# The last batch's down projection as seven products over pairs of d_ff blocks, in an attention and bilinear feed-forward kernel

## The chip, the core and the metric

The kernel is one program on one core of a Trainium2 chip. The core has five engines with queues of their own: TensorE (PE, matrix products into PSUM), VectorE (DVE), ScalarE (ACT), GpSimd (POOL) and SyncE (SP, which here only issues transfers). PEld in a profile is PE's loading of weights, beside its products. Each engine takes its instructions in the order in which the program lists them and waits where one of them needs another engine's result. The metric is the device time of one execution in microseconds, lower is better; several executions of each kernel are timed.

## What is computed

Windowed causal attention with a linear bias, and then a bilinear feed-forward layer on its output:

```python
batch, n_heads, seq, head_dim = (8, 8, 576, 64)
n_tokens, d_model, d_ff = (4608, 512, 1536)

scores = scale * np.matmul(q, k.transpose(0, 1, 3, 2))
mask = (rel >= 0) & (rel < window)          # window 128
scores = np.where(mask, scores + bias[None], -1000000000.0)
attn = softmax(scores)
x = np.matmul(attn, v)                       # heads side by side: 4608 x 512

a = x @ w_a
b = x @ w_b
return (a * b @ w_out).astype(np.float32)
```

All inputs are float32. The kernel reaches that precision with 16-bit operands: a number is kept as a high half (the number rounded to float16) and a low half (what the rounding left), and a product of two numbers is three products: high by high, high by low and low by high.

## The kernel before

**Tiling.** The work goes by batches of 576 tokens (`B` = 8 of them, numbered 0 to 7), d_ff in 12 blocks of 128 (`f`), d_model in 4 blocks of 128. A batch's tokens are two halves `t` of 288 (`HT`). For each batch there is an up stage, which forms the hidden block `a * b` of each `f`, and a down stage, which multiplies the hidden blocks by `w_out`. Attention of a later batch runs in pieces between the steps of both stages (`weave`, `Pace`), so that PE has products of the feed-forward while ACT and DVE do the softmax. The steps of PE stand in the order in which the code is written. The other engines' instructions are placed by a scheduler, which goes by its own account of when each will be ready; `tc.high_priority` moves an instruction ahead. Once placed, the order on each engine is fixed.

**The up stage.** `up_fast` (L853) forms one block `f` in seven steps rather than eight, from sums of weights and sums of inputs that are made ahead. Each step is six products of 288 columns into a PSUM bank (`ch` or `p`), and a bank is read by ACT or DVE before a later step adds to it. The first step of a block goes into `ch`; ACT copies it out at L861; the third step adds to the same bank. The other readers are L868, L884, L889 and L896 on DVE, L873 and L879 on ACT, and L891 on POOL multiplies two of the results. `halve` (L828) then splits the finished hidden block: ACT writes the high half (L829) and DVE the low half (L830) of `h`. Two blocks are in flight, in two lanes.

**The down stage.** For each half `t` and each of the four blocks `e` of d_model, `down` (L925) adds 36 products (12 blocks `f`, three products each) into one bank; ACT scales the bank into `row` (L937) and issues its transfer to the output (L938).

**Between the last attention and the last up stage.** Attention for batch 7 ends inside the down stage of batch 6: PE forms `x_ps` (L501), ACT brings it to `v` (L414), POOL forms differences of its parts (L449, L452, L454, L459) and adds up squares (L430), ACT and DVE split the results into the high and low halves `xs` (L435, L436), PE adds up squares into `n_ps` (L515), and DVE derives scales from them (L516 to L522, and `out_scale`, L944 to L946). From then on no attention is left: the up and down stages of batch 7 run alone.

**Memory.** `wup` and `wdn` hold the weights as float16 halves; `sums_of_weights` (L234) makes the sums for `up_fast` early in the program, POOL adding the halves to float32 (L247), and ACT and DVE splitting the sums again (L256, L257). `work.tile` with a tag reuses a fixed set of buffers; an instruction that writes a reused buffer waits for the last reader of the old contents.

## Time and profile before

| | us |
|---|---|
| median of 3 executions | 1005.48 |
| lowest and highest | 1005.28, 1111.78 |
| the profiled execution | 1006.61 |
| its span, first to last instruction | 1004.80 |
| busy in the span: PE, DVE, ACT, POOL | 965.3, 673.8, 649.2, 307.2 |

The profiled execution took 1.13 us more than the median; 1.81 us of it lie outside the span. Its mean granted TensorE clock is 0.988.

A row of a timeline has the start in us, the time taken in us, the engine, the line, the operation, what it writes and reads with shapes, how many instructions stand in the row, and in brackets for how long its engine had been idle before it and what ended that. A row of the groups has the mean time of one in ns behind the total busy time. A row of the windows has the busy time of each engine in a stretch, with the number of instructions, and the granted TensorE clock (PEclk, 1.00 is full).

### The profile page before, as it was taken

To read this page: it belongs to the slowest core of one execution; us is meant where nothing else is said; L and a number is where in the kernel's file an instruction comes from. 1 tells how busy PE (TensorE), PEld (TensorE's weight loads), DVE (VectorE), ACT (ScalarE), POOL (GpSimd) and SP (SyncE) were. 2 spreads that over 40 slices of the span, in tenths; PEclk is the share of its full clock that TensorE was granted. 3 is DMA by queue.
4 is the path that set the end of the run, shared out by engine and by line. 5 is a ranking of instruction groups with operands and counts; after the bars stand their busy time and mean duration, and the time that the engine had idled before them with its cause. 6 is when DMAs were issued, how large, how long until landed. Compare 5 with 4: busy or idle time off the path is not lost.

```text
span 1004.8 us, 23888 instructions
## 1 busy us (share of the span) xinstructions
PE 965.3 (96%) x9339; PEld 750.9 (75%) x9339; DVE 673.8 (67%) x1833; ACT 649.2 (65%) x1715; POOL 307.2 (31%) x345
## 2 busy tenths in 40 slices
PE   7789879999999999999999999999999999999998
PEld 6567656777777777777787777777777777877776
DVE  5888999657878566775878687666677476524530
ACT  6886779657767756777767767677666766413321
POOL 3643463104565321352226112230223022211100
PEclk7799999999999999999999999999999999999999
DMA  8317733564444442472624642464326632210001
GB/s 318 119 74 266 234 112 73 124 166 81 100 90 96 141 90 43 97 172 66 126 49 107 172 90 45 95 178 107 80 62 106 161 67 43 49 37 7 2 13 36
DMA packets 148433, 102.83 MB, mean 102 GB/s; under 512 B 120032, under 2 KB 128352, under 8 KB 147296
## 3 DMA queue, kind: packets, MB, share of 16 engines
q1 hardware_dynamic: 138816, 91.77, 37.6%
q10 hardware_dynamic: 9504, 9.54, 2.9%
q8 instruction: 73, 1.20, 0.5%
q14 instruction: 40, 0.33, 0.1%
HBM read 48.33 MB, written 9.44 MB: 57 GB/s over the span
## 4 chain that ended last, share of the span: by engine, by line
PE 62%; DVE 11%; DMA 6%; ACT 6%; issue 2%; POOL 1%; SPq 0%; ACTq 0%; DVEq 0%
PE ch L836 19%; PE dn_ps L932 16%; PE p L836 14%; PE up_ps L836 8%; PE x_ps L501 3%; PE sc_ps L378 3%; DVE phl L400 2%; DMA pT<-phl 2%; DMA v<-in_vP 1%; DMA qk<-in_kT 1%; ACT phl L399 1%; DVE t L382 1%; ACT t L383 1%; DVE xs L436 1%; DMA qst<-qkl 1%
## 5 line engine op out<-in xcount | busy, mean ns | idle before, releaser
L836 PEld LDWEIGHTS <-wup 128*128 128x128 f16 x4224 | 407.9, 98 | 120.5 <-issue 14.8
L932 PE MATMUL dn_ps<-h,wdn 128*128 128x288 f16 x2016 | 254.3, 286 | 0.0
L932 PEld LDWEIGHTS <-wdn 128*128 128x128 f16 x2016 | 193.9, 98 | 51.8
L836 PE MATMUL ch<-xs,wup 128*128 128x288 f16 x1536 | 221.7, 286 | 0.9 <-ACT rc L861 0.6
L836 PE MATMUL up_ps<-xs,wup 128*128 128x288 f16 x1536 | 195.1, 286 | 6.1 <-DVE rc L785 4.6
L836 PE MATMUL p<-xs,wup 128*128 128x288 f16 x1152 | 172.6, 286 | 0.0
L891 POOL TENSOR_TENSOR rc<-rc,row 128x288 f32<-128x288 f32 x64 | 62.4, 975 | 279.7 <-DVE row L889 263.8
L400 DVE SCALAR_TENSOR_TENSOR phl<-t,rin,phl 128x192 f16<-128x192 f32 (+2 forms) x252 | 110.0, 477 | 18.9 <-ACT phl L399 18.7
L383 ACT ACTIVATE t<-t,mn 128x192 f32<-128x192 f32 (+2 forms) x252 | 107.2, 427 | 23.4 <-DVE mn L382 23.0
L829 ACT CAST h<-rc 128x576 f16<-128x576 f32 x96 | 64.2, 669 | 68.2 <-DVE rc L896 37.5
L399 ACT ACTIVATE phl<-t,rin 128x192 f16<-128x192 f32 (+2 forms) x252 | 88.7, 425 | 23.3 <-DMA pT<-phl 11.1
L830 DVE TENSOR_TENSOR h<-rc,h 128x576 f16<-128x576 f32 x90 | 71.2, 791 | 32.8 <-ACT h L829 32.0
L382 DVE CUSTOM_DVE_ANT_0 t<-sc_ps,bias,neg 128x192 f32<-128x192 f32 (+2 forms) x216 | 73.7, 389 | 8.4 <-PE sc_ps L378 8.4
L135 POOL TENSOR_TENSOR wup<-wup,wdn 128x512 int32<-128x512 int32 x36 | 54.7, 1541 | 45.6 <-ACT wdn L130 13.2
L937 ACT ACTIVATE row<-dn_ps,oi 128x288 f32<-128x288 f32 x56 | 27.7, 494 | 56.0 <-PE dn_ps L932 55.9
L873 ACT ACTIVATE row<-ch,g 128x288 f32<-128x288 f32 x64 | 31.9, 498 | 48.8 <-PE ch L836 48.8
L436 DVE TENSOR_TENSOR xs<-v,xs 128x576 f16<-128x576 f32 x52 | 48.4, 944 | 21.9 <-ACT xs L435 21.8
L360 POOL TENSOR_SCALAR bias<-rel_sb,ninv,sl_sb 128x192 f32<-128x192 f32 x24 | 21.4, 892 | 123.7 <-DVE mn L382 123.7
L868 DVE TENSOR_TENSOR rc<-p,rc 128x288 f32<-128x288 f32 x64 | 29.1, 454 | 44.1 <-PE p L836 34.8
L896 DVE SCALAR_TENSOR_TENSOR rc<-rc,g,ch 128x288 f32<-128x288 f32 x64 | 32.6, 510 | 23.6 <-PE ch L836 23.4
L383 ACT ACTIVATION_READ_ACCUMULATOR t<-t,mn 128x1 f32 x252 | 47.7, 189 | 0.0
L430 POOL TENSOR_TENSOR xq<-xq,sq 128x576 bf16<-128x576 bf16 x22 | 29.5, 1343 | 56.1 <-ACT sq L429 56.1
(151 smaller groups left out, 1311.7 us busy)
## 6 DMA issues: line engine op xcount, KB each, us to landing
v<-in_vP SPq DMA_DIRECT2D x8, 1280.0 KB, 6.0
out<-row ACTq DMA_DIRECT2D x60, 144.0 KB, 1.8
qk<-in_qT SPq DMA_DIRECT2D x28, 288.0 KB, 4.0
qk<-in_kT SPq DMA_DIRECT2D x28, 288.0 KB, 4.5
wdn<-in_w_a SPq DMA_DIRECT2D x12, 512.0 KB, 5.2
wdn<-in_w_b SPq DMA_DIRECT2D x12, 512.0 KB, 6.2
wdn<-in_w_out SPq DMA_DIRECT2D x12, 512.0 KB, 4.3
qst<-qkh SPq DMA_DIRECT2D x24, 144.0 KB, 2.8
```

Source lines behind the costliest of these rows:

```text
L135: pool.tensor_tensor(out=t[:, m, :], in0=t[:, m, :], in1=low[:, m, :], op=ALU.add)
L382: vec.tensor_tensor_reduce(out=t[:, c:c + w], in0=ps[:, c:c + w], in1=o.bias[:, WIN - w:WIN], scale=-0.125 if o.b == 1 else o.neg, scalar= ...
L383: act.activation(t[:, c:c + w], t[:, c:c + w], AF.Exp, bias=o.mn[:, n:n + 1], scale=-1.0, accum_out=o.sm[:, n:n + 1])
L399: act.activation(phl[:, 0, pc:pc + w], e, AF.Copy, scale=s)
L400: vec.scalar_tensor_tensor(out=phl[:, 1, pc:pc + w], in0=e, scalar=s, in1=phl[:, 0, pc:pc + w], op0=ALU.mult, op1=ALU.subtract)
L436: vec.tensor_tensor(out=xs[:, n, 1, :, :], in0=src, in1=xs[:, n, 0, :, :], op=ALU.subtract)
L829: act.copy(h[:, f, :, 0, :], hid)
L830: eng.tensor_tensor(out=h[:, f, :, 1, :], in0=hid, in1=h[:, f, :, 0, :], op=ALU.subtract)
L836: pe.matmul(ps[:, 0:HT], wup[:, a[0], a[1], wi, k, :], xs[:, b, xi, k, :], start=(first and n == 0), stop=(last and n == len(ks) - 1), ski ...
L891: pool.tensor_tensor(out=x0, in0=x0, in1=mid, op=ALU.mult)
L896: vec.scalar_tensor_tensor(out=x1, in0=x1, scalar=st.g, in1=ch, op0=ALU.mult, op1=ALU.mult)
L932: pe.matmul(ps[:, 0:HT], wdn[:, f, wi, e * P:(e + 1) * P], h[:, f, t, hi, :], start=(m == 0 and n == 0), stop=(m == NF - 1 and n == 2))
```

## The change

In batch 7 alone, the hidden blocks are taken in pairs (`f` even and `f` + 1). For a pair the weights of d_model's two halves form a two by two array of blocks, and so do the hidden blocks over the tokens' two halves. The eight products of these arrays are replaced by seven, whose operands are sums: `Pairs.operands` numbers them 0 to 6. Products 0, 1, 2 take the weights as they are, products 3 to 6 take sums of weights; products 2 to 5 take sums of hidden blocks (`tops`).

`Pairs.weights` makes the sums of weights for six pairs: two POOL additions per pair join the float16 halves to float32 (L968), four DVE operations form the four sums of 256 columns (L970 to L973), and ACT (L980) and DVE (L981) split two tiles of them into halves, twice each. It is written into the second half of batch 6's down stage (6 of its 14 steps) and the first part of batch 7's up stage (8 steps). Its buffers are those that attention has left: `phl`, `pT` and `t` hold the results, `vhl`, `qkh` and `qkl` the float32 values on the way, two of each.

`Pairs.keep` takes the place of `halve` in batch 7: for an even block it splits one half of the tokens, for an odd one it splits both and forms the three sums in place (L995, L997, L998), which are then split (L1000, L1002) into the up weights of block `f` - 1, no longer needed. The hidden blocks themselves are kept in `v` and `qk` instead of the `rc` buffers.

`down_fast` takes the place of `down` in batch 7. For each block `j` of two it adds products 0 and 1 of the first five pairs in banks `dch` and `dp2`, then those of the last pair, then products 5, 4, 3, 2 and 6 of all pairs; ACT and DVE read the banks in between (L1039 to L1058) and ACT issues the transfers of the four results.

```diff
     def up_fast(st, f, h):
...
-        hid, mid = new_hidden(), row()
+        hid, mid = pairs.hidden(f) if h is None else new_hidden(), row()
...
-            halve(hid, f, h, vec)
+            if h is None:
+                pairs.keep(f)
+            else:
+                halve(hid, f, h, vec)
...
+        def weights(self):
+
+            pT = new_pT().rearrange("p a c -> p (a c)")
+            places = [phl[:, n, m:m + 1024] for n in range(2) for m in (0, 1024)] + [pT[:, m:m + 1024] for m in range(0, 4096, 1024)]
+            places += [work.tile([P, 512], F32, tag="t", name="t_ws", bufs=4).bitcast(F16) for _ in range(4)]
+            late = []
+            for i in range(NF // 2 + 1):
+                if i < NF // 2:
+                    a = [work.tile([P, 2, VCOLS], F16, tag="vhl", name="vhl_ws", bufs=2).rearrange("p h c -> p (h c)").bitcast(F32)[:, 0:DM] for _ in range(2)]
...
+                    for n in range(2):
+                        pool.tensor_tensor(out=a[n], in0=wdn[:, f + n, 0, :], in1=wdn[:, f + n, 1, :], op=ALU.add)
+                    a11, a12, a21, a22 = a[0][:, 0:256], a[1][:, 0:256], a[0][:, 256:512], a[1][:, 256:512]
+                    vec.tensor_tensor(out=zs[0][:, 0, :], in0=a21, in1=a22, op=ALU.add)
+                    vec.tensor_tensor(out=zs[1][:, 0, :], in0=a11, in1=a21, op=ALU.subtract)
+                    vec.tensor_tensor(out=zs[0][:, 1, :], in0=zs[0][:, 0, :], in1=a11, op=ALU.subtract)
+                    vec.tensor_tensor(out=zs[1][:, 1, :], in0=a12, in1=zs[0][:, 1, :], op=ALU.subtract)
+                    late.append((i, zs))
+                yield
+                if i:
...
+                    for z, w in zip(zs, self.sums[n]):
+                        act.copy(w[:, :, 0, :], z)
+                        vec.tensor_tensor(out=w[:, :, 1, :], in0=z, in1=w[:, :, 0, :], op=ALU.subtract)
+                yield
...
+        def keep(self, f):
+
+            h, x = self.h, self.fp32[f // 2 % 3]
+            if f % 2 == 0:
+                act.copy(h[:, f, 0, 0, :], x[:, 0, :])
+                vec.tensor_tensor(out=h[:, f, 0, 1, :], in0=x[:, 0, :], in1=h[:, f, 0, 0, :], op=ALU.subtract)
+                return
+            act.copy(h[:, f, :, 0, :], x[:, 2:4, :])
+            vec.tensor_tensor(out=x[:, 0:2, :], in0=x[:, 1:4:2, :], in1=x[:, 0:2, :], op=ALU.subtract)
+            vec.tensor_tensor(out=h[:, f, :, 1, :], in0=x[:, 2:4, :], in1=h[:, f, :, 0, :], op=ALU.subtract)
+            vec.tensor_tensor(out=x[:, 3, :], in0=x[:, 3, :], in1=x[:, 0, :], op=ALU.subtract)
+            vec.tensor_tensor(out=x[:, 2, :], in0=x[:, 2, :], in1=x[:, 3, :], op=ALU.subtract)
...
+            act.copy(tops[:, :, 0, :], x)
+            for n in (0, 2):
+                vec.tensor_tensor(out=tops[:, n:n + 2, 1, :], in0=x[:, n:n + 2, :], in1=tops[:, n:n + 2, 0, :], op=ALU.subtract)
...
+    def down_fast(b, oi, p):
...
+        for n, banks in enumerate((chs, p2s)):
+            for j in range(2):
+                p.product(banks[j], n, j, True, False, early)
+                yield
+        for n, banks in enumerate((chs, p2s)):
+            for j in range(2):
+                p.product(banks[j], n, j, False, True, (NF // 2 - 1,))
...
+        for j in range(2):
+            ch, one, two = chs[j], new_hidden(), new_hidden()
+            (x0, x1), (x2, x3) = ([x[:, n, :] for n in range(2)] for x in (one, two))
+            act.activation(x0, ch, AF.Copy, scale=oi)
+            vec.scalar_tensor_tensor(out=x0, in0=p2s[j], scalar=oi, in1=x0, op0=ALU.mult, op1=ALU.add)
+            out(j, 0, x0)
+            p.product(ch, 5, j, False, True)
+            act.activation(x2, ch, AF.Copy, scale=oi)
+            yield
...
+            p.product(ch, 6, j, False, True)
+            act.activation(x3, ch, AF.Copy, scale=oi)
+            out(j, 1, x3)
+            yield
...
     def batch(b):
...
+        if b == B - 1:
+            pairs.room()
+            weave(up(states[b], None, plain, fast), (halved, 2, 50, 8))
+            for _ in halved:
+                pass
+            for _ in down_fast(b, out_scale(states[b]), pairs):
+                pass
+            return
         weave(att.along(up(states[b], h, plain, fast), n, NPAIR * b + 4), *((spread, *x) for x in quota[b][0]))
-        weave(att.along(down(b, out_scale(states[b]), h, plain + fast), 48, NPAIR * b + 6), *((spread, *x) for x in quota[b][1]))
+        weave(att.along(down(b, out_scale(states[b]), h, plain + fast), 48, NPAIR * b + 6), *((spread, *x) for x in quota[b][1]), *[(halved, 26, 48, 6)] * (b == B - 2))
```

Where the new work stands on the engines is not plain from the code, since the scheduler places it. Three places follow. In the names, `rc` is a hidden block of the kernel before, `v_hid` and `qk_hid` are hidden blocks of batch 7 now; `vhl_ws`, `qkh_ws` and `qkl_ws` are the float32 values of the sums of weights; `phl`, `pT` and `t_ws` as outputs of L980 and L981 are the sums' halves. A line number of the down stage's and `out_scale`'s instructions is another than before (L937 and L938 are now L940 and L941).

POOL, from the last block of batch 6's up stage to batch 7's, before:

```order
L449 TENSOR_TENSOR v<-v 128x2x288
L891 TENSOR_TENSOR rc<-rc,row 128x288
L452 TENSOR_TENSOR v<-v 128x2x288
L430 TENSOR_TENSOR xq<-xq,sq 128x576
L454 TENSOR_TENSOR v<-v 128x2x288
L459 TENSOR_TENSOR v<-v 128x2x288
L891 TENSOR_TENSOR rc<-rc,row 128x288 x12
```

And the same stretch now:

```order
L449 TENSOR_TENSOR v<-v 128x2x288
L891 TENSOR_TENSOR rc<-rc,row 128x288
L968 TENSOR_TENSOR vhl_ws<-wdn 128x512
L452 TENSOR_TENSOR v<-v 128x2x288
L430 TENSOR_TENSOR xq<-xq,sq 128x576
L454 TENSOR_TENSOR v<-v 128x2x288
L968 TENSOR_TENSOR vhl_ws<-wdn 128x512 x2
L459 TENSOR_TENSOR v<-v 128x2x288
L968 TENSOR_TENSOR vhl_ws<-wdn 128x512 x8
L891 TENSOR_TENSOR v_hid<-v_hid,row 128x288 x4
```

Eleven of the twelve additions stand here (the first is further ahead, in batch 6's up stage), and the first product of batch 7's up stage on POOL, L891, stands behind all of them. The first of the eleven waits for PE's last reading of its buffer in `x_ps`.

DVE, from the maximum over `n_ps` to the first reading of a bank of batch 7's up stage, before:

```order
L516 TENSOR_REDUCE xtop<-n_ps 128x1 x2
L518 TENSOR_SCALAR x_13189<-xtop 128x1
L520 TENSOR_SCALAR x2e<-x_13189 128x1
L522 TENSOR_SCALAR g<-x2e 128x1
L944 TENSOR_SCALAR oi<-g,smin,so 128x1
L945 TENSOR_SCALAR oi<-oi,sv 128x1
L946 RECIPROCAL oi<-oi 128x1
L868 TENSOR_TENSOR rc<-p_13386,rc 128x288
```

The end of that stretch now, with the sums of the last two pairs:

```order
L970 TENSOR_TENSOR qkh_ws<-vhl_ws 128x256
L972 TENSOR_TENSOR qkh_ws<-qkh_ws,vhl_ws 128x256
L973 TENSOR_TENSOR qkl_ws<-vhl_ws,qkh_ws 128x256
L981 TENSOR_TENSOR t_ws<-qkh_ws,t_ws 128x2x256
L971 TENSOR_TENSOR qkl_ws<-vhl_ws 128x256
L981 TENSOR_TENSOR t_ws<-qkl_ws,t_ws 128x2x256
L970 TENSOR_TENSOR qkh_ws<-vhl_ws 128x256
L972 TENSOR_TENSOR qkh_ws<-qkh_ws,vhl_ws 128x256
L973 TENSOR_TENSOR qkl_ws<-vhl_ws,qkh_ws 128x256
L981 TENSOR_TENSOR t_ws<-qkh_ws,t_ws 128x2x256
L981 TENSOR_TENSOR t_ws<-qkl_ws,t_ws 128x2x256
L868 TENSOR_TENSOR v_hid<-p_13430,v_hid 128x288
```

All of the sums' work on DVE stands ahead of the first reading of a bank of the last up stage.

ACT, from the last two results of batch 6's down stage to the first copies of batch 7's up stage, before:

```order
L937 ACTIVATE row<-dn_ps,oi 128x288
L938 DMA out<-row 128x288
L937 ACTIVATE row<-dn_ps,oi 128x288
L938 DMA out<-row 128x288
L861 COPY rc<-ch 128x288
L873 ACTIVATE row<-ch,g 128x288
```

And now:

```order
L980 CAST t_ws<-qkh_ws 128x2x256
L980 CAST t_ws<-qkl_ws 128x2x256
L980 CAST t_ws<-qkh_ws 128x2x256
L940 ACTIVATE row<-dn_ps,oi 128x288
L980 CAST t_ws<-qkl_ws 128x2x256
L941 DMA out<-row 128x288
L940 ACTIVATE row<-dn_ps,oi 128x288
L941 DMA out<-row 128x288
L861 COPY v_hid<-ch 128x288
L873 ACTIVATE row<-ch,g 128x288
```

The casts of the last pair's sums stand around the seventh result of the down stage, and L861, on which the third step of the last up stage waits, stands behind them.

More of the change, by code (lines that the diff above doesn't have):

```diff
@@ L995, in attention_then_bilinear_ffn @@
     spread = sums_of_weights()
+    pairs = Pairs(h)
+    halved = pairs.weights()
     quota = [((), ()), (((8, 48, 9),), ((0, 48, 4),)), (((0, 24, 3),), ((0, 48, 5),)), ((), ((0, 48, 4),))] + [((), ())] * (B - 4)
@@ L1008, in batch @@
         n = 4 * len(plain) + 7 * len(fast)
+        if b == B - 1:
[6 more added lines that the diff above has]
+            return
         weave(att.along(up(states[b], h, plain, fast), n, NPAIR * b + 4), *((spread, *x) for x in quota[b][0]))
-        weave(att.along(down(b, out_scale(states[b]), h, plain + fast), 48, NPAIR * b + 6), *((spread, *x) for x in quota[b][1]))
-        if b + 1 < B:
-            assert b + 1 in states
+        weave(att.along(down(b, out_scale(states[b]), h, plain + fast), 48, NPAIR * b + 6), *((spread, *x) for x in quota[b][1]), *[(halved, 26, 48, 6)] * (b == B - 2))
+        assert b + 1 in states
     with tc.manual_schedule(engines=SP):
```

46 lines of the change are left out of this document (added).

## The prediction

> **What bounds the kernel now.** I read the page's busy times first, then the windows of the last three stages, then the end of the chain of waits.
>
> ```profile
> PE 965.3 (96%) x9339; PEld 750.9 (75%) x9339; DVE 673.8 (67%) x1833; ACT 649.2 (65%) x1715; POOL 307.2 (31%) x345
> ```
>
> ```profile
> core 0: us, PE busy (x) PEld busy (x) DVE busy (x) ACT busy (x) POOL busy (x), PEclk, DMA share, GB/s
> 867.00:904.20 37.20, 37.20 (x335) 29.73 (x333) 10.64 (x18) 8.73 (x17) 7.53 (x5) 1.00 0.17 45
> 904.20:966.00 61.80, 61.80 (x506) 49.25 (x504) 30.12 (x57) 22.43 (x48) 8.76 (x11) 1.00 0.01 4
> 966.00:1001.50 35.50, 35.50 (x290) 28.13 (x288) 1.70 (x4) 4.18 (x8) 0.80 (x1) 1.00 0.09 30
> ```
>
> ```profile
> 966.24 35.29 PE dn_ps L932 x288
> 1001.53 0.03 issue
> 1001.55 0.50 ACT row L937
> ```
>
> The three windows are batch 6's down stage, batch 7's up stage and batch 7's down stage. PE is busy in all of each, at full clock, and the chain runs through its products to the last result. So a product less there is worth its pace, 35.29 / 288 = 0.1225 us; and any wait put into PE there is lost in full. DVE, ACT and POOL have room on average.
>
> **The products.** Seven products of six pairs, two blocks and three terms are 252 where 288 stood: 36 x 0.1225 = 4.41 us less. This is certain. The tail is the same: one ACT reading, one transfer of the same size.
>
> **The last down stage** has PE wait for no reader: between two uses of a bank stand the 18 products of another, 2.2 us, against one reading of 0.50 us (the row above). The forming of the last pair's sums is covered by the 72 products of operands 0 and 1, 8.8 us; worked out from the rows below, it takes about 6 (L994 0.67 or L995 0.76, L996 0.76, L997 and L998 0.46 each, L1000 at most twice L829's, 1.3, L1002 1.5). If it took longer, the excess would be lost once. I cost both at nothing.
>
> **The last up stage.** These are the groups of that window, DVE, ACT and POOL:
>
> ```profile
> L830 DVE TENSOR_TENSOR h<-rc,h 128x576 f16<-128x576 f32 x11 | 8.3, 758 | 4.2 <-ACT h L829 4.0
> L889 DVE SCALAR_TENSOR_TENSOR row<-p,g,row 128x288 f32<-128x288 f32 x11 | 5.7, 514 | 1.7 <-PE p L836 1.7
> L896 DVE SCALAR_TENSOR_TENSOR rc<-rc,g,ch 128x288 f32<-128x288 f32 x11 | 5.7, 514 | 11.2 <-PE ch L836 11.2
> L884 DVE TENSOR_TENSOR rc<-ch,rc 128x288 f32<-128x288 f32 x12 | 5.5, 458 | 3.0 <-PE ch L836 3.0
> L868 DVE TENSOR_TENSOR rc<-p,rc 128x288 f32<-128x288 f32 x12 | 5.5, 457 | 27.4 <-PE p L836 27.4
> ```
>
> ```profile
> L829 ACT CAST h<-rc 128x576 f16<-128x576 f32 x11 | 7.4, 672 | 13.8 <-DVE rc L896 13.8
> ```
>
> ```profile
> L891 POOL TENSOR_TENSOR rc<-rc,row 128x288 f32<-128x288 f32 x11 | 8.8, 796 | 69.8 <-DVE row L889 69.8
> ```
>
> Two blocks take PE 61.8 / 6 = 10.3 us. DVE has 2 x (0.457 + 0.458 + 0.514 + 0.514) = 3.9 us of readings there, and 1.5 for two L830. The two L830 go; in come L992 (0.46), L995 (0.76), L996 (0.76), L997 and L998 (0.46 each), two L1002 (0.76 each): 4.4 us. DVE then has 8.3 of 10.3, and if POOL's two L891 (1.6) hold it up in full, 9.9. It fits, with 0.4 us to spare: cost nothing, and a rival below. ACT gets 1.0 us more per two blocks and has room.
>
> **The sums of weights.** This decides. DVE forms with two operands in SBUF, and POOL reading SBUF, do not run beside each other in this trace. First the two operations that L968 and L981 repeat, L247 and L257, where they meet; then how long each takes otherwise (minimum/median/maximum in ns):
>
> ```profile
> 335.06 2.72 POOL L247 TENSOR_TENSOR wup<-wup 128x512 f32<-128x512 f16 x2
> ...
> 335.88 0.89 DVE L257 TENSOR_TENSOR wup<-wup 128x512 f16<-128x512 f32 x1 [1.39 <-ACT wup L256]
> ```
>
> ```profile
> L247 POOL TENSOR_TENSOR wup<-wup x16: 1150/1156/1606, 227.5 to 372.7; 128x512 f32<-128x512 f16 x16
> ```
>
> ```profile
> L257 DVE TENSOR_TENSOR wup<-wup x16: 679/693/1694, 245.8 to 422.3; 128x512 f16<-128x512 f32 x16
> ```
>
> Alone, the three take 1.156 + 0.693 + 1.156 = 3.0 us; together they took 2.72. So they went one after the other, with an overlap of 0.14 at each change of turn. The same can be seen right where the new work goes:
>
> ```profile
> 875.28 1.54 PE L501 MATMUL x_ps<-pT,vhl 128*64 128x128 f16 x42
> ...
> 877.53 1.41 POOL L452 TENSOR_TENSOR v<-v 128x576 f32<-128x576 f32 x1 [8.47 <-ACT v L414]
> ...
> 878.01 3.96 DVE L436 TENSOR_TENSOR xs<-v,xs 128x576 f16<-128x576 f32 x3 [7.45 <-ACT xs L435]
> ...
> 878.89 1.79 POOL L430 TENSOR_TENSOR xq<-xq,sq 128x576 bf16<-128x576 bf16 x1
> ...
> 883.31 1.41 POOL L459 TENSOR_TENSOR v<-v 128x576 f32<-128x576 f32 x1
> ...
> 886.13 0.81 DVE L516 TENSOR_REDUCE xtop<-n_ps 128x1 f32<-128x512 f32 x2
> ...
> 886.98 0.21 DVE L518 TENSOR_SCALAR x<-xtop 128x1 f32<-128x1 f32 x1
> ...
> 887.61 0.27 DVE L944 TENSOR_SCALAR oi<-g,smin,so 128x1 f32<-128x1 f32 x1
> ```
>
> Three L436, of the same shape as L830 (0.758), took 3.96 us, not 2.3, while POOL's L452 and L430 were in their way.
>
> POOL's first L968 of this stretch starts when `x_ps` ends, 876.8. From there on both engines alternate, because each pair's L968 needs the buffers that DVE frees in the pair before, and DVE needs POOL's results. The sum to the last L973:
> - POOL: 11 L968 x 1.156 = 12.7; L452, L430, L454, L459 at 1.41 each, 5.6.
> - DVE, two operands in SBUF: 23 of L970 to L973. No row shows this shape; L830 and L257 give (758 - 693) / 64 = 1.0 ns an element, so 256 elements take 0.693 - 0.26 = 0.43 us, and 23 take 9.9. By bounds it is 0.27 (no fixed part) to 0.69 (L257's): 6.2 to 15.9. I take 0.43, since both rows lie on its line. Five L436 x 0.758 = 3.8. Ten L981 x 0.693 = 6.9.
> - DVE's scales, between them in its queue: about 2.0 (L516 0.81, and six small ones of 0.15 to 0.27).
>
> Together 40.9 us in 53 turns. Neighbours on one engine overlap a little less than 0.14, so I take off 0.1 a turn, 5.3: 35.6, and the last L973 ends at 912.4. Now the boundary of the stages:
>
> ```profile
> 904.40 0.50 ACT L937 ACTIVATE row<-dn_ps,oi 128x288 f32<-128x288 f32 x1 [3.91 <-PE dn_ps L932]
> 904.93 0.34 ACTq L938 DMA_DIRECT2D out<-row  x1
> 904.93 0.90 PE L836 MATMUL p<-xs,wup 128*128 128x288 f16 x6
> 905.31 0.40 ACT L861 COPY rc<-ch 128x288 f32<-128x288 f32 x1 [0.41 <-PE ch L836]
> 905.76 0.90 PE L836 MATMUL ch<-xs,wup 128*128 128x288 f16 x6
> ```
>
> ```profile
> L256 ACT CAST wup<-ws x8: 604/606/615, 432.9 to 573.3; 128x512 f16<-128x512 f32 x8
> ```
>
> PE's third step starts 0.05 us after L861 ends. In the new order L861 stands behind the last pair's two casts (0.61 each, by L256's form), two results (0.50 each) and two issues (0.34 each). The first cast can start at the end of L972, 0.43 ahead of the last L973; 2.9 us, less 0.05 to 0.1 at each step, put L861 2.3 us behind that L973: 914.7 where it was 905.31. **PE waits 9.4 us.** The bounds: with the small DVE price 5.7, with the large one 15.4, with none of the overlap 14.7. The first L968 and L971 stand in batch 6's up stage, where L971 puts at most its 0.43 us ahead of a reading on DVE; PE comes back to that bank two steps (1.5 us) later, so I cost it at nothing.
>
> The Trainium skill, page "SBUF — State Buffer", section "Who interferes with whom", says that a DVE instruction with two SBUF inputs contends with a GpSimd instruction that reads SBUF, and that the one that comes second blocks until the other has finished. The rows agree but for the overlap of 0.14 us; by the page's whole instructions the sum would be 40.9, and the wait 14.7 instead of 9.4. It is the rule that speaks against this change.
>
> **The clock.** A wait of 9 us has a second price. The trace of before shows what PE's clock does after a long pause, early in the program (the first rows are its work, the second the windows):
>
> ```profile
> 64.02 0.41 PE L515 MATMUL n_ps<-sq,ones 128*128 128x512 bf16 x2
> 67.57 0.61 PE L156 MATMUL wn_ps<-wdn,ones 128*128 128x256 bf16 x4 [3.14 <-DVE mn L382]
> ```
>
> ```profile
> 65.09:68.50 3.41, 0.93 (x12) 0.70 (x14) 2.60 (x8) 2.04 (x5) 0.66 (x1) 1.00 0.00 0
> 68.50:71.92 3.42, 3.42 (x29) 2.45 (x26) 0.82 (x2) 1.68 (x5) 0.00 (x0) 0.50 0.00 0
> 71.92:75.33 3.41, 3.41 (x31) 2.31 (x30) 3.41 (x12) 3.13 (x6) 0.72 (x3) 1.00 0.02 5
> ```
>
> After a pause of 3.14 us the granted clock was 0.50 for 3.41 us, all of them busy, and then full. A pause of 9.4 us holds at least one such stretch whole, so PE resumes at 0.50 and stays there for the rest of the stretch in which it resumes (0 to 3.41) and one busy one: 3.4 to 6.8 us, half of which is lost. 1.7 to 3.4; I take **2.4**.
>
> **The sum.** -4.4 + 9.4 + 2.4 = +7.4 us. The profiled execution of 1006.61 (span 1004.80) becomes 1014.0; it was 1.13 above the median of 1005.48, so against the median the change gives **1012.9**, 0.7% slower.
>
> **Rivals.**
> - No wait, so faster than before. If DVE and POOL ran beside each other, POOL's 18.3 us end at 895.1; with four waits of about 1.0 for buffers (L970, L972) and the last three sums (1.3) the last L973 ends at 900.4. It decides at 905.31 - 2.3 = 903.0: any L973 ahead of that leaves only the 4.4 us, 1001.1. The rows at 335 and 878 speak against it; for it, that no DVE row has two float32 operands in SBUF. 6%.
> - The wait without the clock: 1005.48 - 4.4 + 9.4 = 1010.5. Against it stands the pause of 3.14 us. 6%.
> - DVE also falls behind in the last up stage. It decides at 0.4 us more per two blocks; with 1.0 more, 0.6 are lost six times, 3.6 us: 1016.5. 7%.
> - No overlap at the turns: a wait of 14.7, 1018.2. 5%.
> - That the products do not become fewer is excluded by the program's order, which has 252.
>
> **How the numbers follow.** The forecast, wait and clock, has 76%. Its own range goes from a wait of 6 and a clock loss of 1.7 (1008.8) to 12 and 3.4 (1016.5). 1007 to 1017 takes in most of the second and third rivals and leaves out the first, the fourth and the wider ends of the forecast, less than 2 in 10. About 2% is what a measurement of this kernel can tell from no change, 20 us: below 985 none of the cases lies, above 1026 only a wait twice as long would: 0.01 faster, 0.96 the same, 0.03 slower.
>
> **What would show it.** Right: in the last up stage one PE gap of 7 to 12 us before its third step, ended by ACT's L861; L968 and L981 well above 1.156 and 0.693 us where they meet; the last L973 near 912; PEclk 0.50 for 3 to 7 us after the gap, then 1.00; the last down stage 36 x 0.1225 shorter and without gaps. Wrong: the last L973 before 903 with L861 on time; a gap elsewhere in the last up stage, ended by DVE, which is the third rival; or gaps between the products of the last down stage.

## The result, and the profile after

| | before | after |
|---|---|---|
| median, us | 1004.96 (6 executions) | 1011.11 (6 executions) |
| lowest, us | 1003.73 | 1010.11 |
| profiled execution, its span | 1006.61, 1004.80 | 1010.70, 1008.9 |

The ratio is 1.0066, with a 95% interval of 1.0053 to 1.0080: the changed kernel is slower by 5 to 8 us, well inside 2%. One of the six executions of the kernel before took 1111.78 us, and the ratio leaves it out. The 36 products are gone from the count on the page:

```profile
PE 964.9 (96%) x9303; PEld 748.9 (74%) x9303; DVE 722.1 (72%) x1905; ACT 660.5 (65%) x1733; POOL 323.6 (32%) x357
```

The windows are again batch 6's down stage, batch 7's up stage and batch 7's down stage, cut at the first product of each:

```profile
core 0: us, PE busy (x) PEld busy (x) DVE busy (x) ACT busy (x) POOL busy (x), PEclk, DMA share, GB/s
865.50:902.63 37.13, 37.13 (x334) 29.66 (x333) 28.12 (x41) 12.51 (x24) 20.36 (x14) 1.00 0.15 38
902.63:974.53 71.90, 63.74 (x506) 50.05 (x504) 51.61 (x96) 29.25 (x58) 12.16 (x14) 0.95 0.02 7
974.53:1005.50 30.97, 30.97 (x254) 24.56 (x251) 7.49 (x14) 5.21 (x9) 0.79 (x1) 1.00 0.10 35
```

The first and the third are full of PE work, as before. The second took 71.90 us, and PE was busy for 63.74 of them. Its length is the yardstick of all that follows: before, its first product started at 904.20 and the last down stage at 966.07, 61.87 us.

```profile
904.20 0.90 PE L836 MATMUL ch<-xs,wup 128*128 128x288 f16 x6
...
966.07 35.44 PE L932 MATMUL dn_ps<-h,wdn 128*128 128x288 f16 x288
```

So the last up stage has become 71.90 - 61.87 = 10.0 us longer. The timeline of PE at its start shows where:

```profile
902.63 0.90 PE L836 MATMUL ch<-xs,wup 128*128 128x288 f16 x6
903.37 0.90 PE L836 MATMUL p<-xs,wup 128*128 128x288 f16 x6
912.42 1.60 PE L836 MATMUL ch<-xs,wup 128*128 128x288 f16 x6 [8.16 <-ACT v_hid L861]
913.82 1.64 PE L836 MATMUL p<-xs,wup 128*128 128x288 f16 x6
915.26 1.33 PE L836 MATMUL ch<-xs,wup 128*128 128x288 f16 x6
916.42 0.90 PE L836 MATMUL p<-xs,wup 128*128 128x288 f16 x6
```

There is one gap, 8.2 us, ahead of the third step, and it is ended by ACT's L861. Behind it the steps last half as long again to nearly twice as long, until 916.42. The windows of the granted clock say why:

```profile
902.63:909.30 6.67, 1.64 (x14) 1.18 (x12) 6.34 (x10) 1.14 (x2) 3.41 (x3) 1.00 0.06 20
909.30:916.12 6.82, 3.69 (x16) 2.30 (x16) 2.50 (x5) 3.29 (x7) 0.00 (x0) 0.50 0.12 43
916.12:930.00 13.88, 13.88 (x115) 11.06 (x114) 8.58 (x17) 5.08 (x11) 1.59 (x2) 1.00 0.01 2
```

PE worked for 3.7 us at half clock (912.42 to 916.12), which loses half of them, 1.85. The gap and the clock make 8.2 + 1.85 = 10.0, the whole of the longer stage. What PE waited for is seen on ACT and DVE, from the timeline of all engines just ahead of the end of the gap:

```profile
909.57 0.62 ACT L980 CAST t_ws<-qkh_ws 128x512 f16<-128x512 f32 x1 [3.56 <-DVE qkh_ws L972]
909.57 0.43 DVE L973 TENSOR_TENSOR qkl_ws<-vhl_ws,qkh_ws 128x256 f32<-128x256 f32 x1
910.10 0.50 ACT L940 ACTIVATE row<-dn_ps,oi 128x288 f32<-128x288 f32 x1
910.49 0.61 ACT L980 CAST t_ws<-qkl_ws 128x512 f16<-128x512 f32 x1
911.06 0.50 ACT L940 ACTIVATE row<-dn_ps,oi 128x288 f32<-128x288 f32 x1
911.98 0.40 ACT L861 COPY v_hid<-ch 128x288 f32<-128x288 f32 x1 [0.41 <-ACT row L940]
```

Before, L861 ran 1.11 us behind the stage's first product (905.31 - 904.20), which would be 903.74 here. But it stands behind two casts of the last pair's sums, and ACT was idle for 3.56 us waiting for DVE to form them. One turn of the loop that delayed the sums, first POOL, then DVE:

```profile
900.26 2.89 POOL L968 TENSOR_TENSOR vhl_ws<-wdn 128x512 f32<-128x512 f16 x2 [1.82 <-DVE qkh_ws L972]
904.98 2.88 POOL L968 TENSOR_TENSOR vhl_ws<-wdn 128x512 f32<-128x512 f16 x2 [1.82 <-DVE qkh_ws L972]
```

```profile
900.80 1.34 DVE L981 TENSOR_TENSOR pT<-qkh_ws,pT 128x512 f16<-128x512 f32 x1 [0.23 <-ACT pT L980]
902.07 1.64 DVE L981 TENSOR_TENSOR pT<-qkl_ws,pT 128x512 f16<-128x512 f32 x1
903.63 0.41 DVE L971 TENSOR_TENSOR qkl_ws<-vhl_ws 128x256 f32<-128x256 f32 x1
903.96 0.41 DVE L970 TENSOR_TENSOR qkh_ws<-vhl_ws 128x256 f32<-128x256 f32 x1
904.41 0.42 DVE L972 TENSOR_TENSOR qkh_ws<-qkh_ws,vhl_ws 128x256 f32<-128x256 f32 x1
904.87 0.42 DVE L973 TENSOR_TENSOR qkl_ws<-vhl_ws,qkh_ws 128x256 f32<-128x256 f32 x1
908.06 0.68 DVE L981 TENSOR_TENSOR t_ws<-qkl_ws,t_ws 128x512 f16<-128x512 f32 x1
```

A pair takes 904.98 - 900.26 = 4.7 us. POOL waits until DVE has read the two buffers (L972 ends it). While POOL reads, a split of DVE that takes 0.68 alone (the row at 908.06) takes 1.34 or 1.64, and POOL's two additions, 1.15 each alone, take 2.89. DVE is idle for only 0.2 us of the 4.7.

The last down stage runs through: its products start at 974.53, and the last row starts at 1004.67 and takes 0.90, so 31.04 us where the 288 products of before took 35.44 (the row at 966.07 above). That is the 4.4 that the change saves.

```profile
974.53 3.84 PE L1018 MATMUL dch<-h,wdn 128*128 128x288 f16 x30
...
1004.67 0.90 PE L1018 MATMUL dch<-h,t_ws 128*128 128x288 f16 x6
```

In sum -4.4 + 8.2 + 1.85 = +5.7 us, against +6.15 between the medians. (In the two profiles the spans differ by 4.1 only, since the last up stage of this execution began 1.57 us earlier than before's. Its start lies between 901.5 and 905.0 in the profiles of this study, and that was not followed further. So stages are compared by their lengths.)

### The profile page after: what moved, and what is told of

The parts are those of the page before. It is cut to its first block, busy times and chain, and to the rows that moved or that the text cites. A ratio compares the mean times of both kernels' runs of the same rounds, so it can differ in the third digit from the quotient of the medians.

```text
span 1008.9 us, 23919 instructions
## 1 busy us (share of the span) xinstructions
PE 964.9 (96%) x9303; PEld 748.9 (74%) x9303; DVE 722.1 (72%) x1905; ACT 660.5 (65%) x1733; POOL 323.6 (32%) x357
## 4 chain that ended last, share of the span: by engine, by line
PE 64%; DVE 12%; ACT 6%; DMA 3%; issue 2%; POOL 1%; ACTq 0%; SPq 0%; DVEq 0%
PE ch L836 18%; PE p L836 13%; PE dn_ps L935 11%; PE up_ps L836 8%; PE dn_ps L812 3%; PE x_ps L501 3%; PE sc_ps L378 3%; DVE phl L400 2%; PE dch L1018 2%; DVE xs L436 2%; DMA v<-in_vP 1%; PE dp L1018 1%; ACT phl L399 1%; DVE t L382 1%; DVE wup L257 1%
## 5 line engine op out<-in xcount | busy, mean ns | idle before, releaser
L935 PE MATMUL dn_ps<-h,wdn 128*128 128x288 f16 x1728 | 218.8, 286 | 0.0
L836 PE MATMUL up_ps<-xs,wup 128*128 128x288 f16 x1536 | 197.7, 288 | 5.8 <-DVE rc L785 4.1
L935 PEld LDWEIGHTS <-wdn 128*128 128x128 f16 x1728 | 165.8, 98 | 44.6
L891 POOL TENSOR_TENSOR rc<-rc,row 128x288 f32<-128x288 f32 x52 | 52.8, 1016 | 204.9 <-DVE row L889 188.9
L829 ACT CAST h<-rc 128x576 f16<-128x576 f32 x84 | 56.1, 668 | 51.6 <-DVE rc L896 23.7
L830 DVE TENSOR_TENSOR h<-rc,h 128x576 f16<-128x576 f32 x78 | 62.3, 798 | 27.4 <-ACT h L829 26.9
L436 DVE TENSOR_TENSOR xs<-v,xs 128x576 f16<-128x576 f32 x52 | 50.9, 990 | 19.8 <-ACT xs L435 19.7
L430 POOL TENSOR_TENSOR xq<-xq,sq 128x576 bf16<-128x576 bf16 x22 | 29.1, 1324 | 51.9 <-ACT sq L429 51.9
L435 ACT CAST xs<-v 128x576 f16<-128x576 f32 x52 | 34.1, 668 | 14.7 <-POOL v L454 6.3
L501 PEld LDWEIGHTS <-vhl 128*64 128x64 f16 x1176 | 40.6, 110 | 4.0 <-issue 3.6
L501 PE MATMUL x_ps<-pT,vhl 128*64 128x128 f16 (+2 forms) x1176 | 42.9, 228 | 0.0
```

Source lines behind the costliest of these rows:

```text
L436: vec.tensor_tensor(out=xs[:, n, 1, :, :], in0=src, in1=xs[:, n, 0, :, :], op=ALU.subtract)
L501: pe.matmul(xp[oc // 512][64 * h:64 * h + 64, o0:o0 + w], vt[0:rows, c:c + 64], probs(pt, rows, blocks, h), start=(n == 0 and first), stop ...
L829: act.copy(h[:, f, :, 0, :], hid)
L830: eng.tensor_tensor(out=h[:, f, :, 1, :], in0=hid, in1=h[:, f, :, 0, :], op=ALU.subtract)
L836: pe.matmul(ps[:, 0:HT], wup[:, a[0], a[1], wi, k, :], xs[:, b, xi, k, :], start=(first and n == 0), stop=(last and n == len(ks) - 1), ski ...
L891: pool.tensor_tensor(out=x0, in0=x0, in1=mid, op=ALU.mult)
```

## The experiments

The theory is the prediction's: the sums of weights go round a loop in which POOL and DVE hinder each other, come late, and ACT's queue puts the copy that PE needs behind their casts. The rivals: the wait is made by the last up stage itself; only the two buffers are short; the slow steps behind the wait have another cause than the clock. The yardstick of each run, worked out from the starts of the stages in its profile:

| kernel | last up stage, us | PE waits in it | median, us |
|---|---|---|---|
| before | 61.87 | none | 1004.96 |
| after | 71.90 | 8.2 | 1011.11 |
| products_alone | 61.93 | none | 1001.07 |
| sums_alone | 71.94 | 8.15 | 1014.97 |
| kept_warm | 70.09 | 0.56 | 1010.01 |
| splits_on_act | 68.78 | 4.8 | 1009.56 (one) |
| four_buffers | 69.70 | 5.6 | 1009.46 (one) |
| all_on_dve | 67.04 | 3.8 | 1006.94 (one) |
| casts_behind | 65.08 | 2.7 | 1005.05 (one) |
| begun_earlier | 71.98 | 8.2 | 1009.69 (one) |
| early_casts | 62.51 | 0.5 | 1001.01 |
| earlier_sums | 61.87 | none | 1000.67 |

The kernel before, measured beside these, had medians of 1005.27 (beside products_alone, sums_alone, kept_warm and splits_on_act), 1004.96 (beside four_buffers, all_on_dve, casts_behind and earlier_sums) and 1006.75 (beside begun_earlier and early_casts). The kernels marked "one" were timed once, so what is read from them is their profile.

### The two halves of the change, each alone

**products_alone**: products 3 to 6 take plain weights, and no sum of weights is formed (its steps in batch 6's down stage, not shown in the cut below, go as well). So the output is another.

```diff
-            return self.sums[i][k % 2][:, k // 2, :, e], (self.tops[i][:, 0], self.tops[i][:, 1], self.tops[i][:, 3], h[:, f + 1, 1])[k]
+            return wdn[:, f + k % 2, :, e], (self.tops[i][:, 0], self.tops[i][:, 1], self.tops[i][:, 3], h[:, f + 1, 1])[k]
...
-            weave(up(states[b], None, plain, fast), (halved, 2, 50, 8))
-            for _ in halved:
-                pass
+            weave(up(states[b], None, plain, fast))
```

> Left out: the sums of weights. No block of the down matrix is added, split or cast; products 3 to 6 of the last down stage take slices of the plain down matrix as weights, so the output is not the reference's. All 252 products, the sums over pairs of d_ff blocks in the last up stage (the DVE work of L1009 to L1013 in the changed kernel) and the three extra buffers stay. Theory (the wait comes from the sums of weights alone, the products save 36 x 0.1225 us): no PE gap before the third step of the last up stage, ACT copies the hidden block right after it is asked to, the last down stage is about 4.4 us shorter than before, time about 1000.5 us, 0.995 to 0.996 of the kernel before. Rival (the wait comes from the last up stage itself, its DVE work or its new buffers): a gap of several us stays somewhere between 900 and 925 us, time 1004 to 1011 us.

Measured: 0.9962 of before (0.9949 to 0.9975), 4.2 us faster. On PE's timeline the third step follows the second at once:

```profile
905.75 0.90 PE L836 MATMUL p<-xs,wup 128*128 128x288 f16 x6
906.63 0.90 PE L836 MATMUL ch<-xs,wup 128*128 128x288 f16 x6
```

So DVE's added work of `Pairs.keep` and the other buffers of the hidden blocks cost next to nothing (the stage is 61.93 us long, 61.87 before), and seven products give what their count says.

**sums_alone**: the sums are formed, and the last batch runs as before.

```diff
-            pairs.room()
-            weave(up(states[b], None, plain, fast), (halved, 2, 50, 8))
+            weave(up(states[b], h, plain, fast), (halved, 2, 50, 8))
...
-            for _ in down_fast(b, out_scale(states[b]), pairs):
+            for _ in down(b, out_scale(states[b]), h, plain + fast):
```

> Changed: the sums of weights are formed as in the changed kernel, in the same steps and buffers, but nothing reads them; the last up stage and the last down stage with eight products are those of the kernel before. Theory: the PE gap of 8 to 9 us before the third step of the last up stage is there, and half clock for 3 to 4 us of work behind it (1.5 to 2.5 us lost), nothing gained by products: 1013 to 1016 us, 1.008 to 1.011 of the kernel before. Rival (the gap comes from the last up stage or its buffers, the sums of weights are covered by other work): no gap, within 1.5 us of the kernel before.

Measured: 1.0099 of before (1.0084 to 1.0114), 9.7 us slower, with the same gap, ended by the same copy (into `rc` here, the buffer of before):

```profile
911.39 1.60 PE L836 MATMUL ch<-xs,wup 128*128 128x288 f16 x6 [8.15 <-ACT rc L861]
```

The two halves add up: -4.2 + 9.7 = +5.5, beside +6.15 for the whole. The first rival falls: the wait is the sums' alone.

### The clock

**kept_warm**: PE is given work that nobody needs during the gap.

```diff
+        if h is None and f == 0:
+            spare = ps_at.tile([P, 512], F32, tag="at", name="spare")[:, 0:HT]
+            for _ in range(62):
+                pe.matmul(spare, wup[:, 0, 0, 0, 0, :], xs[:, 0, 0, 0, :], start=True, stop=True)
```

> Added: 62 products of 128 x 257 into a spare PSUM bank that nothing reads, ahead of the third step of the last up stage, so that PE is busy for about 7.6 us of its 8.2 us wait. Theory (what follows the wait costs because of the clock alone): the third step starts when it did, at the end of the same ACT copy, but runs and is followed at full clock; the stretch behind the wait is 1.5 to 2.2 us shorter, time 1.5 to 2.2 us below the changed kernel's. Rival (the steps behind the wait are slow because they wait for DVE or ACT, which are late themselves): the steps behind the wait stay 1.3 to 1.6 us, time unchanged or longer.

PE's timeline, with the 62 products in the gap:

```profile
905.55 7.76 PE L874 MATMUL spare<-xs,wup 128*128 128x288 f16 x62
913.87 0.90 PE L836 MATMUL ch<-xs,wup 128*128 128x288 f16 x6 [0.56 <-ACT v_hid L861]
```

The third step starts 913.87 - 904.09 = 9.78 us behind the first, as in the changed kernel (912.42 - 902.63 = 9.79), but runs at full pace. The stage is 71.90 - 70.09 = 1.8 us shorter. That is the price of the clock. The ratio to before, 1.0047 (1.0031 to 1.0064), has an interval that overlaps the changed kernel's, so it is the profile that shows this, not the timing.

### What makes the sums late

**splits_on_act**: DVE's two splits of a pair are taken away from it; ACT writes a second copy where the low half would stand, so the output is another.

```diff
-                        vec.tensor_tensor(out=w[:, :, 1, :], in0=z, in1=w[:, :, 0, :], op=ALU.subtract)
+                        act.copy(w[:, :, 1, :], z)
```

> Changed: the second half of each split weight (the difference on DVE, 128 x 512, two a pair) becomes a plain copy on ACT, so the low halves hold wrong values and the output is not the reference's. POOL's two sums and DVE's four of each pair stay. Theory (POOL's and DVE's operations on SBUF take turns, their sum sets the pace of a pair, and ACT's queue then holds the hidden copy back): a pair loses two DVE turns of 0.68 us, its period falls from 4.7 us to 3.3 to 3.9 us, the last sum of weights ends 4 to 6 us earlier against the start of the last up stage, and the PE gap falls from 8.2 to 2.5 to 5.5 us. Rival (POOL alone sets the pace, or each step waits for the one before it through two buffers): the period stays within 0.3 us of 4.7 and the gap stays 7 to 9 us.

The same loop on POOL, two turns:

```profile
898.81 2.44 POOL L968 TENSOR_TENSOR vhl_ws<-wdn 128x512 f32<-128x512 f16 x2 [1.23 <-DVE qkh_ws L972]
902.47 2.44 POOL L968 TENSOR_TENSOR vhl_ws<-wdn 128x512 f32<-128x512 f16 x2 [1.22 <-DVE qkh_ws L972]
```

A pair takes 3.7 us in place of 4.7, and POOL's two additions 2.44 in place of 2.89: taking work from DVE made POOL faster. The last L973 ends 2.4 us behind the start of the stage (906.02 + 0.42 - 904.02) where it was 7.4 (910.00 - 902.63), and the gap fell to 4.8. All as the theory had it. But ACT now has four casts a pair, so of the 5.0 us by which the sums came earlier 3.4 reached PE.

**four_buffers**: POOL need not wait for DVE's reading of the pair before.

```diff
-                    a = [work.tile([P, 2, VCOLS], F16, tag="vhl", name="vhl_ws", bufs=2).rearrange("p h c -> p (h c)").bitcast(F32)[:, 0:DM] for _ in range(2)]
+                    a = [work.tile([P, 2, VCOLS], F16, tag="vhl", name="vhl_ws", bufs=2).rearrange("p h c -> p (h c)").bitcast(F32)[:, 0:DM] if i % 2 == 0 else work.tile([P, 2, HT], F32, tag="rc", name="rc_ws", bufs=3).rearrange("p h c -> p (h c)")[:, 0:DM] for _ in range(2)]
```

> Changed: the POOL sums of every second pair go into two buffers of the pool rc in place of the two of the pool vhl, so that a pair's POOL work need not wait until DVE has read the pair before it. Nothing else changes. Theory (POOL and DVE take turns at SBUF, and the sum of their turns sets the pace of a pair): POOL starts a pair earlier, but its additions then meet DVE's four sums, which take longer for it; the last sum of weights ends only 1 to 3 us earlier against the start of the last up stage and the PE gap stays 5 to 7.5 us. Rival (the two buffers make the loop of POOL and DVE that takes 4.7 us a pair): the period falls to 3.6 us or less and the gap to 0 to 3 us.

The gap came out as expected, 5.6 us, but the way to it did not. The last L973 ended 5.2 us earlier against the start of the stage, not 1 to 3. The edit did more than it was meant to: three of the additions, those into `rc`, now ran ahead of `x_ps`, behind which eleven of the twelve stand in the changed kernel (in this run POOL goes on from `x_ps` at 876.31).

```profile
859.55 1.15 POOL L968 TENSOR_TENSOR rc_ws<-wdn 128x512 f32<-128x512 f16 x1 [2.39 <-DVE rin L396]
...
866.71 1.15 POOL L968 TENSOR_TENSOR rc_ws<-wdn 128x512 f32<-128x512 f16 x1 [0.69 <-DVE h L830]
...
870.70 1.15 POOL L968 TENSOR_TENSOR rc_ws<-wdn 128x512 f32<-128x512 f16 x1 [1.58 <-DVE h L830]
```

One L971 more ran ahead of it too, and two more of the splits L981 fell behind the last L973. Three additions of 1.15, one L971 of 0.42 and two splits of 0.68 are 5.2 us of turns, less about 0.1 at each, which is most of what was gained. So the two buffers cost above all by holding back the start of the sums. That the loop itself became shorter is not shown by this run, and the rival's gap of 0 to 3 us did not come. (PE waited 0.3 us in batch 6's down stage, for an L830 of DVE, which it does not in the changed kernel.) What then held L861 back was ACT's order, as its timeline shows:

```profile
907.08 0.49 ACT L940 ACTIVATE row<-dn_ps,oi 128x288 f32<-128x288 f32 x1
...
908.04 0.50 ACT L940 ACTIVATE row<-dn_ps,oi 128x288 f32<-128x288 f32 x1 [0.47 <-ACT row L940]
...
909.46 0.50 ACT L940 ACTIVATE row<-dn_ps,oi 128x288 f32<-128x288 f32 x1 [0.92 <-DMA out<-row]
...
910.37 0.40 ACT L861 COPY v_hid<-ch 128x288 f32<-128x288 f32 x1 [0.41 <-ACT row L940]
```

Three results of the down stage had piled up behind the casts, the last of which ended at 907.16, and the third even waited 0.92 us for a row buffer.

**all_on_dve**: POOL has no part in the sums.

```diff
-                        pool.tensor_tensor(out=a[n], in0=wdn[:, f + n, 0, :], in1=wdn[:, f + n, 1, :], op=ALU.add)
+                        vec.tensor_tensor(out=a[n], in0=wdn[:, f + n, 0, :], in1=wdn[:, f + n, 1, :], op=ALU.add)
```

> Changed: the two additions of 128x512 a pair go to DVE in place of POOL, so POOL forms no sums of weights. Theory (POOL in its turns keeps DVE from working, so its share of the work saves nothing): an addition on DVE takes about 0.7 us (as the split of the same tile) in place of POOL's 1.15 to 1.47, no operation of DVE is stretched to 1.3 us or more, a pair takes 4.1 to 4.6 us in place of 4.7, the gap is 3 to 7 us. Rival (POOL's share is real parallel work, and only the two buffers and their loop are slow): DVE's own work of a pair grows by 1.4 us on top of the loop, a pair takes over 5 us, and the gap grows to 11 us or more.

DVE's timeline, one pair and the start of the next:

```profile
899.09 1.29 DVE L968 TENSOR_TENSOR vhl_ws<-wdn 128x512 f32<-128x512 f16 x2
900.29 0.69 DVE L981 TENSOR_TENSOR pT<-qkh_ws,pT 128x512 f16<-128x512 f32 x1
...
903.09 1.29 DVE L968 TENSOR_TENSOR vhl_ws<-wdn 128x512 f32<-128x512 f16 x2
```

A pair takes 4.0 us with DVE doing everything, less than the 4.7 with POOL's help (and a little less than my 4.1 to 4.6), and the gap is 3.8. POOL's two additions a pair cost DVE 0.66 + 0.96 = 1.6 us in stretched splits (1.34 and 1.64 where one takes 0.68), while making both itself costs 1.29. Help that takes turns with the helped engine is no help here.

### Where the casts stand in ACT's queue

**casts_behind**: the casts are ordered behind the last copy out of PSUM.

```diff
-                        act.copy(w[:, :, 0, :], z)
+                        with tc.issue_after(last_main[0].ins):
+                            act.copy(w[:, :, 0, :], z)
```

> Changed: each ACT cast of a sum of weights is put in ACT's order behind the last copy that empties a PSUM bank at the place where it is written, so the copies of the last up stage no longer stand behind the last pairs' casts. POOL's and DVE's work on the sums is as before and in the same order among itself. Theory (the gap is the ACT queue: the hidden copy is ready and stands behind casts that wait for late sums): the one gap of 8 us breaks up into several of 0.5 to 3.5 us that sum to 3 to 5 us, most of the loss of clock goes with it, and the time is 3 to 6 us below the changed kernel's. Rival (PE waits because the sums themselves are late, in whatever order ACT has them): 8 us or more of waits, in the last up stage or ahead of the products 3 to 6 of the last down stage.

What PE waited for from batch 6's down stage on (total, times, longest):

```profile
PE ch L836 <- DVE v_hid L896: 2.3, 2, 2.1
PE ch L836 <- ACT v_hid L861: 0.4, 1, 0.4
```

The stage fell from 71.90 to 65.08 us by the order of the casts. (DVE's order moves with ACT's, since a split of L981 needs its cast: here DVE's first reading of a bank, L868, stands ahead of the last pairs' sums, at 906.59.) The waits sum to 2.7, a little under the 3 to 5 expected, and the one execution took 6 us less than the changed kernel's median. What is left is another wait: more of the sums now fall into the last up stage, DVE there is busy for 9.21 of the 10 us from 925 to 935, and PE waits 2.1 us for its L896. This is the prediction's third rival, made to happen by loading DVE further.

**begun_earlier**: only the steps of the code are moved ahead.

```diff
-            weave(up(states[b], None, plain, fast), (halved, 2, 50, 8))
+            weave(up(states[b], None, plain, fast), (halved, 2, 50, 3))
...
-        weave(att.along(down(b, out_scale(states[b]), h, plain + fast), 48, NPAIR * b + 6), *((spread, *x) for x in quota[b][1]), *[(halved, 26, 48, 6)] * (b == B - 2))
+        weave(att.along(down(b, out_scale(states[b]), h, plain + fast), 48, NPAIR * b + 6), *((spread, *x) for x in quota[b][1]), *[(halved, 0, 48, 11)] * (b == B - 2))
```

> Changed: only the places in the code at which the steps of the sums are written: 11 of 14 in the down stage of batch 6 from its first product on, in place of 6 from the 26th, and 3 in place of 8 in the last up stage. Theory (POOL's sums need the buffers vhl, which attention gives back at its last product, x_ps, and POOL and DVE then go round one loop): nothing starts earlier, the gap stays within 1 us of the changed kernel's 8.2 us. Rival (the sums are late because their steps are written late): the gap falls to 4 us or less.

Nothing changed: the gap is 8.2 us, the stage 71.98. POOL's addition waits for PE's `x_ps` just as in the changed kernel:

```profile
874.24 1.15 POOL L968 TENSOR_TENSOR vhl_ws<-wdn 128x512 f32<-128x512 f16 x1 [7.84 <-PE x_ps L501]
```

**early_casts**: both of these edits together, with the changed kernel's buffers.

> Changed: the casts of the sums are put behind the last copy out of PSUM in ACT's order, as in the kernel with the casts behind, and the steps are written earlier, as in the kernel begun earlier; the buffers are the changed kernel's. Theory (what costs is where the casts stand in ACT's order against the copies of the last up stage, not the buffers): more casts now stand ahead of the stage and fewer sums fall into it, so PE waits 0.5 to 2.5 us in it and no wait is long enough to lower the clock, 1000.5 to 1003 us. Rival (without other buffers the sums cannot be ready in time): waits of 4 us or more, 1005 us or more.

Measured: 1001.01 us, 0.9951 of the kernel before (0.9933 to 0.9969). ACT's timeline at the start of the stage:

```profile
903.39 0.40 ACT L861 COPY v_hid<-ch 128x288 f32<-128x288 f32 x1 [0.41 <-PE ch L836]
```

L861 is again released by PE itself. One wait of 0.5 us is left, for L879. DVE still forms all of the sums ahead of its first reading of a bank (the splits of the last two pairs come later):

```profile
908.12 0.42 DVE L973 TENSOR_TENSOR qkl_ws<-vhl_ws,qkh_ws 128x256 f32<-128x256 f32 x1
908.47 0.82 DVE L868 TENSOR_TENSOR v_hid<-p,v_hid 128x288 f32<-128x288 f32 x2
```

The last L973 ends 6.3 us behind the start of the stage (at 902.27), nearly as late as the 7.4 of the changed kernel, and L868 begins 6.2 us behind it, and still PE waits only those 0.5 us. So late sums alone, and DVE's readings behind them, do not make a wait of 8 us. (In the changed kernel DVE's last split ahead of L868 ends at 911.8, 9.2 us behind the start. What that would cost with ACT's copy on time was not tried.) Neither edit does this alone; with the steps written earlier, "the last copy" that a cast is put behind is an earlier one, so that more pairs are done ahead of the stage, and those that are late no longer stand in its way.

**earlier_sums**: the sums begun with the down stage of batch 6, in other buffers.

```diff
-                    a = [work.tile([P, 2, VCOLS], F16, tag="vhl", name="vhl_ws", bufs=2).rearrange("p h c -> p (h c)").bitcast(F32)[:, 0:DM] for _ in range(2)]
+                    a = [work.tile([P, 2, HT], F32, tag="rc", name="rc_ws", bufs=3).rearrange("p h c -> p (h c)")[:, 0:DM] for _ in range(2)]
...
-                        pool.tensor_tensor(out=a[n], in0=wdn[:, f + n, 0, :], in1=wdn[:, f + n, 1, :], op=ALU.add)
+                        with tc.issue_after(last_mul[0].ins):
+                            pool.tensor_tensor(out=a[n], in0=wdn[:, f + n, 0, :], in1=wdn[:, f + n, 1, :], op=ALU.add)
...
-                        act.copy(w[:, :, 0, :], z)
+                        with tc.issue_after(last_main[0].ins):
+                            act.copy(w[:, :, 0, :], z)
```

The steps are written as in begun_earlier, `t` comes first among the places of the results, and `last_mul` is the last L891.

> Changed: the sums of weights begin with the down stage of batch 6 (11 of the 14 steps in it, from its first product on, in place of 6 from the 26th), with POOL's results in two buffers of the pool rc, the four small buffers t for the first pairs; POOL's additions stand behind the last gating product that POOL has at that place, ACT's casts behind the last copy out of PSUM. The output is the reference's. Theory (the same turns, but begun some 15 us earlier, end before the last up stage needs ACT and DVE): no PE gap of over 1 us in the last two stages, the products' 4.4 us are kept, time 1000 to 1002 us, 0.995 to 0.997 of the kernel before. Rival (the stretch ahead has no room either: POOL's turns then delay the norm and the casts of x for the last batch, or the attention's softmax): a new gap of 2 us or more at the start of the last up stage or in the down stage of batch 6, time 1003 us or more.

Measured: 1000.67 us, 0.9952 of before (0.9938 to 0.9965). The stage is 61.87 us long, as before the change; PE waits for nothing in the last three stages.

```profile
904.10 0.90 PE L837 MATMUL p<-xs,wup 128*128 128x288 f16 x6
904.92 0.90 PE L837 MATMUL ch<-xs,wup 128*128 128x288 f16 x6
```

It and early_casts reach what products_alone allows, 1001.07. Each is 4 to 6 us faster than the kernel before measured beside it, and some 10 faster than the changed one, and there is next to nothing more to win from the sums.

## Why the prediction was right

It said 1012.9 us, from 1007 to 1017, and 1011.11 came. Step by step:

- **The products**: 4.41 predicted; 4.40 in the profile (35.44 to 31.04 us of last down stage) and 4.2 timed by themselves. Right.
- **The last down stage**: no gap, as predicted. The last pair's sums were taken to need 6 us; from L896 at 974.73 to the end of the last L1002 at 980.5 they took 5.8, under the 8.8 of cover. (The prediction's own terms add up to 5.2; from L995 at 975.28, where they begin, it was 5.3.)
- **The last up stage**: 8.3 of 10.3 us of DVE per two blocks were predicted; 7.9 of 10.29 were measured from 920.83 on, and products_alone ran it without a gap. The third rival was no more than possible, and needed casts_behind's load to appear.
- **The sums of weights**: 35.6 us predicted from the first addition to the last L973; 34.7 measured (875.34 to 910.00). The unknown price, an operation of 128x256 on DVE, was taken as 0.43; it is 0.41 to 0.43 where POOL is not in the way. (Beside POOL's L430 the first L971 took 1.49 us, where the prediction put 0.43 at most; no wait of PE followed, as it had taken.)
- **The wait**: 9.4 predicted, 8.2 measured: 0.9 of the difference is in that sum, 0.3 in the way from the last L973 to L861 (2.0 for 2.3; that part was added up wrongly, since 2.9 less 0.43 and six steps of 0.05 to 0.1 is 1.9 to 2.2). It is the term that was sized most wrongly, and still within its bounds.
- **The clock**: 2.4 predicted, 1.85 measured, by the mechanism stated: the rest of the stretch in which PE resumes (0.3 us) and one whole stretch of 3.41.
- **What the prediction left out**: it put the lateness down to turns at the SBUF and named ACT's order only as the way from the last sum to L861. The runs give that order the greater weight: with the same operations on POOL and DVE and the same buffers, the order of the casts with the steps written earlier brought the stage from 71.90 to 62.51 us. The late sums are needed only in the last down stage; it was the queue that made them urgent. The two buffers count above all for when the sums can begin (begun_earlier, four_buffers); the gain in four_buffers is little more than the turns that it moved out of the way.

The Trainium skill, page "SBUF — State Buffer", section "Who interferes with whom", has the second of two such instructions wait for the whole of the first. The runs agree in kind (splits of 1.34 and 1.64 us where 0.68 is needed; POOL faster when DVE has less to do). With whole turns the wait would have been 14.7 us by the prediction's estimate, where 8.2 was measured, so the overlap at each change of turn matters for the size.

## What to carry to other kernels

A saving on the engine that bounds the kernel is only kept if what it needs is not queued, on some other engine, ahead of a reading that this engine waits for: look at what stands before each copy out of PSUM once the new work is placed, and keep work that is needed later behind it. Price a pair of engines that hinder each other as one engine, and try the helped engine alone: here DVE by itself was faster than DVE and POOL together. A gap of PE of several us costs more than its length, since the clock falls and takes a while to come back: here 1.85 us on top of 8.2.

## What was not expected of the hardware

The clock fell at places where PE had not paused for a whole stretch. Two neighbouring windows of the changed kernel, early in the program:

```profile
131.06:134.47 3.41, 1.21 (x10) 0.83 (x9) 3.41 (x6) 1.06 (x2) 2.41 (x2) 1.00 0.76 294
134.47:137.88 3.41, 3.30 (x14) 1.92 (x15) 3.41 (x16) 3.41 (x14) 1.28 (x1) 0.50 0.64 220
```

PE was busy for 1.21 of the 3.41 us of the first, and the clock was 0.50 in the next. The prediction's own row shows the same: the stretch from 65.09 holds 0.93 us of work. The traces of before and after, cut into stretches of this length from end to end, give the share roughly: at full clock, every stretch with 1.76 us of work or more was followed by full clock and every one with 1.41 or less by 0.50, and from 1.64 to 1.74 both occur. And two independent operations of 128x256 follow each other on DVE in 0.33 us (L971 at 903.63, L970 at 903.96), while one that needs the result before it comes 0.46 behind it (L972 at 904.41, L973 at 904.87): 0.13 us a dependence. In four_buffers, where DVE takes two pairs in turn, it is not paid (two L972 at 904.33 and 904.67).
